# An x eviction on VectorE, a normalisation on GpSimd, and weight tiles split earlier

## The chip, the cores and the metric

The kernel runs on one core of one Trainium2 chip. The metric is the device time of one launch in microseconds (us). Before the change it was 877.35 us, the median of three runs (876.28 to 878.45). The engines are called PE (TensorE, matrix products), ACT (ScalarE), DVE (VectorE), POOL (GpSimd) and SP (SyncE, which here only issues DMAs). SBUF is the on-chip memory, PSUM the banks into which PE accumulates.

## The reference

Three stages follow one another, with B = 4, H = 8 heads of 64, 512 local and 32 global tokens for each batch.

```python
# 1. attention: local queries see a band of +-32 keys and the 32 global keys, global queries see all
out_g = sm(scale * q_g @ k_all.T) @ v_all
out_l = sm(concat(scale * q_l @ k_g.T, where(|i-j| <= 32, scale * q_l @ k_l.T, -1e9))) @ concat(v_g, v_l)
x = concat(out_g, out_l)                       # 2176 tokens x 512
# 2. gated layer, 512 -> 1536 -> 512
x = ((sigmoid(x @ w_gate) * (x @ w_val)) @ w_out)
# 3. routed layer: tokens with x @ w_skip > 0 go to the best of 8 experts (512 -> 1024 -> 512), the others pass
out = x;  out[sel] += gate_w * (relu(x[sel] @ w1[e]) @ w2[e])
```

The weights of the gated layer come as 64-bit numbers. They are turned into 32-bit words on the chip ("narrowed"), scaled by a power of two, and split into a high and a low 16-bit part, so that a product is made of three matmuls.

## The kernel before, in words

**Attention (to about 177 us).** There are 32 units, one for each tile of 128 tokens and each half of the heads. A software pipeline, written out in `MAIN` (L57), runs in each step u the scores of unit u, the softmax of the units before, the transposes of unit u-3, the value products of unit u-4, and the eviction `xout` of unit u-5. The eviction (`x_out`, L431) copies two halves of 64 partitions x 256 from PSUM (`xo`) to SBUF (`xT`) and then stores the tile; `ENG` (L55) says which engine makes each half (`x0`, `x1`: 'a' is ACT, 'v' DVE, 'p' POOL). For each batch and half of the heads the global queries have steps of their own (`globals_`, L444): a maximum, an exponential, the normalisation `norm` (L464, 128x544, engine `g_n`), transposes of it by PE (`tpg`), and value products (`xog`).

**Side steps.** Weight tiles of the gated layer are made inside the pipeline. Tile n (of 12) has three raw pieces of 512 KB, k = 3n to 3n+2 (gate, value, output). A piece is fetched (L140, SP), narrowed (three DVE passes, L156, L158, L160); of the first two the absolute sum is taken by ACT (`total_w1`, L177, output `junk`, sums in `vm`), summed over partitions by a small PE matmul (`sum_w1`, L180, output `ws`), turned into scales (`scale_w1`, four small DVE operations from L170 to L172 and L533), and split: the high part by ACT (`high_w1`, L102, `wa`, `wb`), the low part as the difference on DVE (`low_w1`, L202) or, for the third piece, on POOL (L109) where `SUBS` says so. `W_FIRST` (L51) holds the steps at which tiles 0 to 4 begin, `W_STEPS` the steps that follow.

**The tail (177 to about 205 us).** `UPS` (L60) puts the up products of weight tiles 0 to 3 for the first token block into the last steps, while the last global queries are finished. An up product of one tile is 24 matmuls of 128x512 (L570 to L572) into two banks `pp` of three; the sigmoid `sg` (ACT, L581), the product `g` (DVE, L583) and its split `gh` (ACT, L596) and `go` (DVE, L597) follow. ACT loads another function table before the first sigmoid.

**Gated layer, first block.** For each of 12 tiles (`fc`) the loop at L983 runs up (L561), gated, cut, then the sum of a later weight tile (`w1_sum`), the down product of the tile before (12 matmuls of 128x512, L609 to L611), and then `w1_make`, which scales and splits that later tile, fetches further pieces, and narrows the tile behind it (`w1_words`). Raw pieces from k = 15 on rotate over 11 places: four of pool `st`, four of `st2`, three of `rw` (L122). Tile 5 is summed and made at fc 0, tile 6 at fc 4, ..., tile 11 at fc 9. Five more token blocks follow, with all weights in place, and then the routed layer to the end of the run. Each engine works through its own instructions in the program's order.

Of the kernel before, what the change touches and what calls it, by code (L numbers as in the profile page):

```python
# [11 lines left out]
F32 = mybir.dt.float32  # L12
# [35 lines left out]
G_STEPS = [[(0, 'top'), (0.5, 'weigh'), (1.5, 'over'), (1.5, 'norm'), (2, 'turn', 0), (2.5, 'turned', 0), (3, 'turn', 1), (3.5, 'turned', 1), (4, 'value'), (4.5, 'out')], [(1, 'top'), (1.5, 'weigh'), (2.5, 'over'), (2.5, 'norm'), (5, 'turn', 0), (5.5, 'turned', 0), (6, 'turn', 1), (6.5, 'turned', 1), (7, 'value'), (7.5, 'out')]]  # L48
G_LAST = [[(0, 'top'), (0, 'weigh'), (0.5, 'over'), (0.5, 'norm'), (1, 'turn', 0), (1, 'turned', 0), (1.5, 'turn', 1), (1.5, 'turned', 1), (2, 'value'), (2.5, 'out')], [(0, 'top'), (0, 'weigh'), (0.5, 'over'), (0.5, 'norm'), (2.5, 'turn', 0), (2.5, 'turned', 0), (3, 'turn', 1), (3, 'turned', 1), (3.5, 'value'), (4, 'out')]]
W_STEPS = [(0, 'fetch', 0), (0.5, 'fetch', 1), (2.5, 'narrow', 0), (3, 'total', 0), (3, 'narrow', 1), (3.5, 'fetch', 2), (3.5, 'total', 1), (5, 'sum'), (5.5, 'scale'), (5.5, 'high', 0), (6, 'low', 0), (6, 'high', 1), (6, 'narrow', 2), (6.5, 'low', 1), (6.5, 'high', 2), (7, 'low', 2)]  # L50
W_FIRST = (4, 10, 16, 22, 28)  # L51
X_STEPS = [(16, 'load'), (17, 'total', 0), (18, 'total', 1), (19, 'total', 2), (20, 'total', 3), (22, 'sum'), (22.5, 'scale'), (23, 'part', 0), (24, 'part', 1), (25, 'part', 2), (26, 'part', 3)]
SUBS = 'vvp'
W_LOW = 'v'
ENG = {'x0': 'a', 'x1': 'a', 'g_n': 'a', 't0': 'a', 't1': 'a', 'tg': 'v'}  # L55

MAIN = [('gout', 1), ('tmm', 3), ('norm', 2), ('score', 0, 0), ('score', 1, 0), ('turned', 3), ('xout', 5), ('exp', 0, 1), ('exp', 1, 1), ('mid',), ('max', 0, 0), ('max', 1, 0), ('gmm', 0), ('val', 4), ('end',)]  # L57
STEPS = 38
TAGS = {'x': 1, 's': 2, 'pr': 3, 'sm': 2, 'pt': 2, 'xT': 2}
UPS = (33, 34, 35, 36)  # L60
EARLY = len(UPS)
# [13 lines left out]
def moe_kernel(ctx, tc, qL, kL, qG, vA, wpack, epack, wr, wrT, masks, cst, out):  # L75
# [46 lines left out]
    place = {}  # L122
    for k in range(W0, 3 * NW):
        i = (k - W0) % (sum(NST) + 3)
        name = "st" if i < NST[0] else "st2" if i < sum(NST) else "rw"
        place[k] = name, [j for j in place if place[j][0] == name]
    for k, (name, prev) in place.items():
        n = dict(rw=3, st=NST[0], st2=NST[1])[name]
# [148 lines left out]
    def at(u, f):  # L277
        if u <= -1:
            f()
        else:  # L280
            side.setdefault(u, []).append(f)
# [333 lines left out]
    def bank(name):  # L615
        banks.append(banks.pop(0))
        return mps.tile([128, 512], F32, tag=banks[-1], name=name)
# [111 lines left out]
        return steps + [r_pick, r_place]  # L729

    todo = []
    w1k = [W0, W0 // 3]

    def w1_fetch(a):

# [4 lines left out]
    def w1_words(n):  # L740
        if n < NW:
            narrow_w1(3 * n, 3 * n + 1)
            narrow_w1(3 * n + 2)
            for k in range(3 * n, 3 * n + 2):
                total_w1(k)

    def w1_sum(n):
        if n < NW:
            w1s.append(bank("ws")[:, 0:2])
            sum_w1(n, w1s[-1])  # L750

    w1s = []
# [1 line left out]
    def w1_make(n):  # L754

        if n >= NW:
            return
        scale_w1(n, w1s.pop())
        for k in range(3 * n, 3 * n + 3):
            high_w1(k)  # L760
        for k in range(3 * n, 3 * n + 3):
            low_w1(k, SUBS[k % len(SUBS)])
        w1_fetch(3 * n + 3)
        w1_words(n + 1)
        if n + 1 == NW:
            st2.close()
            pools["wpc"] = ctx.enter_context(tc.tile_pool(name="wpc", bufs=4, reuse_waits="tile"))
            st.close()
            pools["wpd"] = ctx.enter_context(tc.tile_pool(name="wpd", bufs=2, reuse_waits="tile"))
# [28 lines left out]

    for n, u0 in enumerate(W_FIRST):
        do = dict(fetch=lambda h, n=n: fetch_w1(3 * n + h), narrow=lambda h, n=n: narrow_w1(3 * n + h), total=lambda h, n=n: total_w1(3 * n + h),  # L800
                  sum=lambda n=n: side_sum(2, lambda ps: sum_w1(n, ps)), scale=lambda n=n: scale_w1(n, summed.pop()),
                  high=lambda h, n=n: high_w1(3 * n + h), low=lambda h, n=n: low_w1(3 * n + h, W_LOW))
        for r, f, *a in W_STEPS:
            at(u0 + r, lambda f=do[f], a=a: f(*a))

    do = dict(load=lambda: x_load(0), total=lambda k: x_total(0, k), sum=lambda: side_sum(4, lambda ps: x_sum(0, ps)),
              scale=lambda: x_scale(0, summed.pop()), part=lambda k: x_part(0, k))
# [37 lines left out]

    st2 = ctx.enter_context(ExitStack())
    pools["st2"] = st2.enter_context(tc.tile_pool(name="st2", bufs=NST[1], reuse_waits="tile"))
    w1_fetch(W0)
    w1_words(W0 // 3)
    mps = mp.enter_context(tc.tile_pool(name="mps", bufs=1, space=PSUM, reuse_waits="tile"))  # L850

    def gather(xr, ix):
# [118 lines left out]
    for n in range(NB):  # L971
        if n == 1:
            xs_ = ctx.enter_context(ExitStack())
            xa = xs_.enter_context(tc.tile_pool(name="xa", bufs=1, reuse_waits="tile"))
            aix = xa.tile([128, NA], I32, tag="aix", name="aix")

            zrows = xa.tile([128, XW], F32, tag="axr", name="zrows", bufs=NA)
            nc.gpsimd.memset(zrows, 0.0)
            w_rows((NE,), xa.tile([128, XW], F32, tag="axr", name="wrow", bufs=NA)[:, 0:512])
            for t in range(first_tile[NB - 1], NT):  # L980
                for r, m, row in token_rows(t):
                    nc.sync.dma_start(x1d[row:row + m, :], zrows[r:r + m])
        for fc in range(NFC):  # L983
            if n or fc >= EARLY:
                up(n, fc)
                gated(n, fc)
                cut(n, fc)
            if n == 0:
                w1_sum(max(fc, 3) + 2 if fc in (0, *range(4, NFC)) else NW)
            if n == NB - 1 and todo and fc >= 1:  # L990
                todo.pop(0)()
            if fc:
                down(n, fc - 1)
            if n == 0 and fc == 1:
                cut(0, 3)
            if n == 0 and fc == NFC - 2:

                for c in range(3):
                    w_rows((2 * c, 2 * c + 1), rw.tile([128, 1024], F32, tag="raw", name="wrow"))
                for c in (6, 7):  # L1000
                    w_rows((c,), rw.tile([128, 512], F32, tag="cut", name="wrow", bufs=2))
            if n == 0:
                w1_make(max(fc, 3) + 2 if fc in (0, *range(4, NFC)) else NW)
            if n + 1 < NB:
                if fc == 2:
                    x_load(n + 1)
                if 4 <= fc < 8:
                    x_total(n + 1, fc - 4)
                if fc == 9:
                    ps = bank("xs")[:, 0:4]  # L1010
                    x_sum(n + 1, ps)
                    x_scale(n + 1, ps)
            if todo and fc >= 1:
                todo.pop(0)()
            if n == NB - 1 and fc < NFC - 1:

                free = NR - 1 + max(0, fc - 1)
                w2_ahead(min(NW + 2 * fc, free - 1, 27), min(free, 27))
        if n + 1 < NB:
            x_split(n + 1)  # L1020
        down(n, NFC - 1)
        todo = route(n)
        if n == NB - 2:
            r_rows, t0, s0, t1, s1, t2, s2, r_pick, r_place = todo
            none = lambda: None
            todo = [r_rows, t0, t1, s0, t2, s1, s2, r_pick, none, r_place, none, a_list, a_gather] + 8 * [none] + [lambda: a_turn(0)]
        if n < NB - 1:
            todo.pop(0)()
# [360 lines left out]
```

## Time and profile before

| | |
|---|---|
| median of three runs | 877.35 us (876.28 to 878.45) |
| the profiled execution | 878.84 us, of which span 877.1 us |
| PE busy | 780.1 us (89%) |
| DVE busy | 505.7 us (58%) |
| ACT busy | 378.7 us (43%) |
| POOL busy | 72.1 us (8%) |
| DMA moved | 105.80 MB, mean 121 GB/s |

The span is the stretch that the profiler saw; the rest of the execution lies around it. The shares are means over the whole run and differ much by stage, so the stages are looked at by stretches, by the waits of PE and by the instructions in their order of time.

### The profile page before, as it was taken

The page shows a single profiled execution, that of the slowest core. Times are in us where ns is not written, and L with a number is a line of the kernel's source. Part 1 is how long each engine was busy: PE and PEld are TensorE (multiplying, and loading weights), DVE is VectorE, ACT ScalarE, POOL GpSimd, SP SyncE. Part 2 cuts the span into 40 slices and gives each one's busy share as a digit, 9 for nine tenths or more (in the row PEclk, how much of TensorE's full clock was granted, in tenths as well). Part 3 has the DMA queues.
Part 4 walks back from the last instruction along what each step waited for, and adds up shares of the span by engine and source line. Part 5 has one row for each costly group of instructions (what it writes and reads, how often), then busy time and mean ns, then how long its engine had stood idle before and what let it go on. Part 6 is the DMA issues. An engine that isn't in the chain of part 4 may idle for free. (4 is left out here: it accounts for less than half of the span.)

```text
span 877.1 us, 13434 instructions
## 1 busy us (share of the span) xinstructions
PE 780.1 (89%) x4598; PEld 595.9 (68%) x4598; DVE 505.7 (58%) x1358; ACT 378.7 (43%) x906; POOL 72.1 (8%) x95
## 2 busy tenths in 40 slices
PE   5989898997978999999999999989987576799993
PEld 5989798964644566666678866667865454578773
DVE  5576878844688557635647755336424266554731
ACT  4596979762244332131232232143423255553530
POOL 2000000000111000010000010100111201132210
PEclk9899999998998999999999999999999687899997
DMA  8988786245430230021011020034718476654300
GB/s 247 233 250 205 253 232 191 70 147 181 143 128 30 73 109 13 5 82 25 0 73 37 17 69 1 25 133 147 154 49 122 163 274 209 221 188 167 114 26 18
DMA packets 58404, 105.80 MB, mean 121 GB/s; under 512 B 10609, under 2 KB 32369, under 8 KB 57282
## 3 DMA queue, kind: packets, MB, share of 16 engines
q1 hardware_dynamic: 52386, 94.47, 36.4%
q0 software_dynamic: 3040, 6.70, 2.4%
q10 hardware_dynamic: 2880, 3.41, 1.4%
q8 instruction: 51, 0.84, 0.4%
q14 instruction: 47, 0.39, 0.2%
HBM read 87.82 MB, written 17.98 MB: 121 GB/s over the span
## 5 line engine op out<-in xcount | busy, mean ns | idle before, releaser
L570 PE MATMUL pp<-xh,wa 128*128 128x384 f16 (+2 forms) x576 | 184.9, 321 | 0.0
L572 PE MATMUL pp<-xh,wa 128*128 128x384 f16 (+2 forms) x576 | 183.9, 319 | 0.0
L571 PE MATMUL pp<-xl,wa 128*128 128x384 f16 (+2 forms) x576 | 183.8, 319 | 0.0
L583 DVE SCALAR_TENSOR_TENSOR g<-pp,inv,sg 128x384 f32<-128x384 f32 (+2 forms) x72 | 42.8, 595 | 116.9 <-PE pp L572 112.2
L581 ACT ACTIVATE sg<-pp,inv 128x384 f32<-128x384 f32 (+2 forms) x72 | 40.5, 562 | 134.8 <-PE pp L572 131.5
L609 PE MATMUL acc<-wb,gh 128*128 128x512 f32 x200 | 89.5, 448 | 0.0
L596 ACT CAST gh<-g 128x384 fp32r<-128x384 f32 (+2 forms) x71 | 35.0, 493 | 122.2 <-DVE g L583 120.8
L570 PEld LDWEIGHTS <-wa 128*128 128x128 f16 x576 | 57.3, 99 | 44.0 <-issue 15.7
L216 DVE TENSOR_TENSOR wb<-raw,wa 128x1024 fp32r<-128x1024 f32 x64 | 76.1, 1221 | 18.4 <-ACT wa L215 17.3
L610 PE MATMUL acc<-wb,gh 128*128 128x512 f32 x200 | 82.1, 411 | 0.0
L611 PE MATMUL acc<-wb,go 128*128 128x512 f32 x200 | 81.9, 410 | 0.0
L572 PEld LDWEIGHTS <-wa 128*128 128x128 f16 x576 | 56.7, 98 | 33.3 <-issue 1.2
L718 DVE CUSTOM_DVE_ANT_0 junk<-x,wrow 128x512 f32<-128x512 f32 x108 | 75.4, 698 | 2.6
L571 PEld LDWEIGHTS <-wa 128*128 128x128 f16 x576 | 56.9, 99 | 29.1 <-issue 0.8
L215 ACT CAST wa<-raw 128x1024 fp32r<-128x1024 f32 x64 | 64.9, 1047 | 14.9 <-DMA raw<-in_epack_dram 13.1
L597 DVE TENSOR_TENSOR go<-g,gh 128x384 fp32r<-128x384 f32 (+2 forms) x71 | 37.9, 534 | 39.0 <-ACT gh L596 38.6
L340 PE MATMUL sp<-k,qz 128*128 128x160 f32 x256 | 45.1, 323 | 12.5 <-DMA x1d<-zrow 5.7
L379 ACT ACTIVATE pr<-sm,st 128x160 f32<-128x160 f32 x128 | 53.2, 417 | 0.7
L424 PE MATMUL xo<-pt,g 128*128 128x128 f32 x256 | 49.8, 276 | 0.0
L340 PEld LDWEIGHTS sp<-k,qz 128*128 128x128 f32 x256 | 39.6, 207 | 13.3 <-issue 5.9
L609 PEld LDWEIGHTS acc<-wb,gh 128*128 128x128 f32 x200 | 39.6, 198 | 11.0 <-issue 1.7
L611 PEld LDWEIGHTS acc<-wb,go 128*128 128x128 f32 x200 | 39.4, 197 | 9.7
(276 smaller groups left out, 1400.4 us busy)
## 6 DMA issues: line engine op xcount, KB each, us to landing
raw<-in_epack_dram SPq DMA_DIRECT2D x64, 512.0 KB, 5.6
raw<-in_wpack_dram SPq DMA_DIRECT2D x36, 512.0 KB, 4.6
k<-in_kL_dram SPq DMA_DIRECT2D x32, 256.0 KB, 6.0
v<-in_vA_dram SPq DMA_DIRECT2D x4, 1280.0 KB
x1d<-x SPq DMA_DIRECT2D x16, 260.0 KB, 2.4
w<-in_vA_dram SPq DMA_DIRECT2D x8, 512.0 KB, 8.3
xTd<-xT SPq DMA_DIRECT2D x16, 256.0 KB, 5.3
out_dram<-x SPq DMA_DIRECT2D x16, 256.0 KB, 4.6
```

The lines of the kernel that those rows point to most:

```text
L215: nc.scalar.copy(t[0], raw)
L216: nc.vector.tensor_sub(t[1], raw, t[0])
L340: nc.tensor.matmul(sp[:, 160 - 160 * s:320 - 160 * s], q, qk[t][g][:, pp, 96 * s:96 * s + 160], start=True, stop=True)
L379: nc.scalar.activation(U[u, "pr"][:, c // 2, cs], sm[:, c // 2, cs], AF.Exp, bias=st[:, c:c + 1], scale=-1.0, accum_out=U[u, "r"][:, c:c + 1])
L424: nc.tensor.matmul(xo[:, pp, s], gf[b % 2][:, s, p], pt[:, 4], start=False, stop=True)
L570: nc.tensor.matmul(pp[:, 0:nt], hi[:, ks], xh[k][:, 0:nt], start=(k == 0), stop=False)
L571: nc.tensor.matmul(pp[:, 0:nt], hi[:, ks], xl[k][:, 0:nt], start=False, stop=False)
L572: nc.tensor.matmul(pp[:, 0:nt], lo[:, ks], xh[k][:, 0:nt], start=False, stop=(k == 3))
L609: nc.tensor.matmul(acc, gh[:, gs], hi, start=(fc == 0), stop=False)
L610: nc.tensor.matmul(acc, gh[:, gs], lo, start=False, stop=False)
L611: nc.tensor.matmul(acc, go[:, gs], hi, start=False, stop=(fc == NFC - 1))
L718: nc.vector.tensor_tensor_reduce(junk, R["x1"][:, g, 0:DM], wrow[c], op0=ALU.mult, op1=ALU.add, scale=1.0, scalar=0.0, accum_out=R["lo"][: ...
```

## The change

Five things change. The second half of each x eviction goes from ACT to DVE (32 copies of 64x256). The normalisation of the global queries goes from ACT to POOL (8 of 128x544), as a multiply by a value per partition. The first two weight tiles of the gated layer begin at steps 2 and 9 instead of 4 and 10. Tiles 5 and 6 are fetched, narrowed, summed and made by entries of a new table `W_TAIL` in the tail (steps 33.5 to 38; one step more is run); in the first block tile 7 is summed and made at fc 0, tiles 8 to 11 at fc 3 to 6, and the narrowing runs two tiles ahead: tiles 7 and 8 are narrowed ahead of the loop, and `w1_make(n)` narrows tile n+2. The raw places rotate as `st`, `rw`, `st2`.

```diff
--- before.py
+++ after.py
@@ -48,14 +48,16 @@
 G_STEPS = [[(0, 'top'), (0.5, 'weigh'), (1.5, 'over'), (1.5, 'norm'), (2, 'turn', 0), (2.5, 'turned', 0), (3, 'turn', 1), (3.5, 'turned', 1), (4, 'value'), (4.5, 'out')], [(1, 'top'), (1.5, 'weigh'), (2.5, 'over'), (2.5, 'norm'), (5, 'turn', 0), (5.5, 'turned', 0), (6, 'turn', 1), (6.5, 'turned', 1), (7, 'value'), (7.5, 'out')]]
 G_LAST = [[(0, 'top'), (0, 'weigh'), (0.5, 'over'), (0.5, 'norm'), (1, 'turn', 0), (1, 'turned', 0), (1.5, 'turn', 1), (1.5, 'turned', 1), (2, 'value'), (2.5, 'out')], [(0, 'top'), (0, 'weigh'), (0.5, 'over'), (0.5, 'norm'), (2.5, 'turn', 0), (2.5, 'turned', 0), (3, 'turn', 1), (3, 'turned', 1), (3.5, 'value'), (4, 'out')]]
 W_STEPS = [(0, 'fetch', 0), (0.5, 'fetch', 1), (2.5, 'narrow', 0), (3, 'total', 0), (3, 'narrow', 1), (3.5, 'fetch', 2), (3.5, 'total', 1), (5, 'sum'), (5.5, 'scale'), (5.5, 'high', 0), (6, 'low', 0), (6, 'high', 1), (6, 'narrow', 2), (6.5, 'low', 1), (6.5, 'high', 2), (7, 'low', 2)]
-W_FIRST = (4, 10, 16, 22, 28)
+W_FIRST = (2, 9, 16, 22, 28)
+
+W_TAIL = [(33.5, 'words', 5), (35, 'fetch'), (35.5, 'sum', 5), (36, 'make', 5), (36.5, 'words', 6), (38, 'sum', 6), (38, 'make', 6)]
 X_STEPS = [(16, 'load'), (17, 'total', 0), (18, 'total', 1), (19, 'total', 2), (20, 'total', 3), (22, 'sum'), (22.5, 'scale'), (23, 'part', 0), (24, 'part', 1), (25, 'part', 2), (26, 'part', 3)]
 SUBS = 'vvp'
 W_LOW = 'v'
-ENG = {'x0': 'a', 'x1': 'a', 'g_n': 'a', 't0': 'a', 't1': 'a', 'tg': 'v'}
+ENG = {'x0': 'a', 'x1': 'v', 'g_n': 'p', 't0': 'a', 't1': 'a', 'tg': 'v'}
 
 MAIN = [('gout', 1), ('tmm', 3), ('norm', 2), ('score', 0, 0), ('score', 1, 0), ('turned', 3), ('xout', 5), ('exp', 0, 1), ('exp', 1, 1), ('mid',), ('max', 0, 0), ('max', 1, 0), ('gmm', 0), ('val', 4), ('end',)]
-STEPS = 38
+STEPS = 39
 TAGS = {'x': 1, 's': 2, 'pr': 3, 'sm': 2, 'pt': 2, 'xT': 2}
 UPS = (33, 34, 35, 36)
 EARLY = len(UPS)
@@ -122,7 +124,7 @@
     place = {}
     for k in range(W0, 3 * NW):
         i = (k - W0) % (sum(NST) + 3)
-        name = "st" if i < NST[0] else "st2" if i < sum(NST) else "rw"
+        name = "st" if i < NST[0] else "rw" if i < NST[0] + 3 else "st2"
         place[k] = name, [j for j in place if place[j][0] == name]
     for k, (name, prev) in place.items():
         n = dict(rw=3, st=NST[0], st2=NST[1])[name]
@@ -729,7 +731,7 @@
         return steps + [r_pick, r_place]
 
     todo = []
-    w1k = [W0, W0 // 3]
+    w1k = [W0]
 
     def w1_fetch(a):
 
@@ -744,9 +746,9 @@
             for k in range(3 * n, 3 * n + 2):
                 total_w1(k)
 
-    def w1_sum(n):
+    def w1_sum(n, ps=None):
         if n < NW:
-            w1s.append(bank("ws")[:, 0:2])
+            w1s.append((bank("ws") if ps is None else ps)[:, 0:2])
             sum_w1(n, w1s[-1])
 
     w1s = []
@@ -761,7 +763,8 @@
         for k in range(3 * n, 3 * n + 3):
             low_w1(k, SUBS[k % len(SUBS)])
         w1_fetch(3 * n + 3)
-        w1_words(n + 1)
+        if n >= NWA:
+            w1_words(n + 2)
         if n + 1 == NW:
             st2.close()
             pools["wpc"] = ctx.enter_context(tc.tile_pool(name="wpc", bufs=4, reuse_waits="tile"))
@@ -802,6 +805,9 @@
                   high=lambda h, n=n: high_w1(3 * n + h), low=lambda h, n=n: low_w1(3 * n + h, W_LOW))
         for r, f, *a in W_STEPS:
             at(u0 + r, lambda f=do[f], a=a: f(*a))
+    do = dict(fetch=lambda: w1_fetch(W0), words=w1_words, sum=lambda n: w1_sum(n, aps.tile([128, 6, 128], F32, tag="tp", name="ws", bufs=1)[:, 0]), make=w1_make)
+    for u, f, *a in W_TAIL:
+        at(u, lambda f=do[f], a=a: f(*a))
 
     do = dict(load=lambda: x_load(0), total=lambda k: x_total(0, k), sum=lambda: side_sum(4, lambda ps: x_sum(0, ps)),
               scale=lambda: x_scale(0, summed.pop()), part=lambda k: x_part(0, k))
@@ -845,8 +851,9 @@
 
     st2 = ctx.enter_context(ExitStack())
     pools["st2"] = st2.enter_context(tc.tile_pool(name="st2", bufs=NST[1], reuse_waits="tile"))
-    w1_fetch(W0)
-    w1_words(W0 // 3)
+    w1_fetch(3 * NWA)
+    w1_words(NWA)
+    w1_words(NWA + 1)
     mps = mp.enter_context(tc.tile_pool(name="mps", bufs=1, space=PSUM, reuse_waits="tile"))
 
     def gather(xr, ix):
@@ -986,7 +993,7 @@
                 gated(n, fc)
                 cut(n, fc)
             if n == 0:
-                w1_sum(max(fc, 3) + 2 if fc in (0, *range(4, NFC)) else NW)
+                w1_sum(NWA + (0, NW, NW, 1, 2, 3, 4, *[NW] * 5)[fc])
             if n == NB - 1 and todo and fc >= 1:
                 todo.pop(0)()
             if fc:
@@ -1000,7 +1007,7 @@
                 for c in (6, 7):
                     w_rows((c,), rw.tile([128, 512], F32, tag="cut", name="wrow", bufs=2))
             if n == 0:
-                w1_make(max(fc, 3) + 2 if fc in (0, *range(4, NFC)) else NW)
+                w1_make(NWA + (0, NW, NW, 1, 2, 3, 4, *[NW] * 5)[fc])
             if n + 1 < NB:
                 if fc == 2:
                     x_load(n + 1)
```

Line numbers of the changed kernel are two to seven higher. On DVE at the end of the tail, before the change, the scales of tile 4 (`we`, `ws`, `inv`) are followed by the copy of the last transposed global weights (`ptg`) and the first gated product (`g`):

```order
519 L170 TENSOR_SCALAR we<-pt 128x2
520 L171 TENSOR_SCALAR we<-we 128x2
521 L172 TENSOR_SCALAR ws<-we 128x2
522 L533 TENSOR_SCALAR inv<-we,xq 128x2
523 L104 COPY ptg<-tpg 128x128
524 L583 SCALAR_TENSOR_TENSOR g<-pp,inv,sg 128x512
```

and after it:

```order
552 L535 TENSOR_SCALAR inv<-we,xq 128x2
553 L158 TENSOR_SCALAR cut<-raw 128x512 x2
554 L160 SCALAR_TENSOR_TENSOR cut<-raw,cut 128x512 x2
555 L162 SCALAR_TENSOR_TENSOR raw<-raw,cut 128x512 x2
556 L158 TENSOR_SCALAR cut<-raw 128x512
557 L160 SCALAR_TENSOR_TENSOR cut<-raw,cut 128x512
558 L162 SCALAR_TENSOR_TENSOR raw<-raw,cut 128x512
559 L106 COPY ptg<-tpg 128x128
560 L585 SCALAR_TENSOR_TENSOR g<-pp,inv,sg 128x512
```

The narrowing of tile 5 (the passes on `cut` and `raw`) now stands between the scales and `ptg`; its sums (ACT `junk`) stand ahead of ACT's table load.

On PE, at the end of the last up product of the tail (`pp`), the sum `ws` and the start of the first down product (`acc`), before:

```order
638 L572 MATMUL pp<-xh_1775,wa 128x512
639 L180 MATMUL ws<-vm,onesf 128x2
640 L609 MATMUL acc_2506<-wb,gh 128x512
641 L610 MATMUL acc_2506<-wb,gh 128x512
642 L611 MATMUL acc_2506<-wb,go 128x512
```

and after:

```order
639 L574 MATMUL pp<-xh_1775,wa 128x512
640 L182 MATMUL ws<-vm,onesf 128x2 x2
641 L611 MATMUL acc_2588<-wb,gh 128x512
642 L612 MATMUL acc_2588<-wb,gh 128x512
643 L613 MATMUL acc_2588<-wb,go 128x512
```

The one sum there was of tile 5; now there are two, of tiles 6 and 7, and the first down product stands behind both.

On DVE in the pipeline of attention, between the normalisation of a unit (`pr`, `pk`) and the masked maximum (`sm`, `st`) of a later one, with the semaphores that an instruction waits for, before:

```order
118 L388 TENSOR_TENSOR pr<-pr,r 128x2x2x128 [waits DVE_49]
119 L391 TENSOR_TENSOR pk<-pr,r 128x128
120 L351 ISA sm,st<-sp,mask_sb 128x160 [waits PE_49]
121 L351 ISA st 128x1
122 L351 ISA sm,st<-sp,mask_sb 128x160
```

and after, where the second half of the eviction (`xT`) has come in, and a low part moved:

```order
129 L390 TENSOR_TENSOR pr<-pr,r 128x2x2x128 [waits DVE_49]
130 L393 TENSOR_TENSOR pk<-pr,r 128x128
131 L106 COPY xT<-xo 64x256 [waits DMAHW6_49,PE_49,Activation_49]
132 L204 SCALAR_TENSOR_TENSOR wa<-raw,ws,wa 128x512
133 L353 ISA sm,st<-sp,mask_sb 128x160 [waits PE_49]
134 L353 ISA st 128x1
```

The new copy waits for PE and for ACT; the maxima stand behind it.

## Rows read from the trace of the kernel before

**Rows 1.** Busy time by stretch (span, then per engine: busy and count); PEclk, DMA share, GB/s.

```profile
125.00:150.00 25.00, 20.37 (x166) 19.39 (x165) 20.59 (x86) 20.06 (x63) 0.00 (x0) 1.00 0.74 219
...
sum 151.00, PE 139.18 PEld 135.23 DVE 114.66 ACT 119.41 POOL 0.00; mean PE 23.20 PEld 22.54 DVE 19.11 ACT 19.90 POOL 0.00
...
200.00:212.00 12.00, 11.40 (x52) 5.86 (x50) 2.19 (x6) 1.30 (x2) 0.00 (x0) 0.86 0.42 112
```

**Rows 2.** PE waits, 24 to 178 us: who waits for whom; total, times, longest.

```profile
PE tpg L471 <- ACT pgf L102: 4.8, 3, 2.3
```

**Rows 3.** The same for PE from 178 to 310 us.

```profile
PE ws L180 <- ACT junk L177: 13.9, 5, 5.0
```

**Rows 4.** DVE groups by form, 0 to 180 us: total busy, mean ns; idle before.

```profile
L104 DVE COPY ptg<-tpg 128x512 f32<-128x512 f32 x6 | 4.1, 683 | 0.0
...
L492 DVE COPY xTg<-xog 64x64 f32<-64x64 f32 x12 | 2.6, 220 | 1.2 <-PE xog L486 1.1
...
L104 DVE COPY ptg<-tpg 128x128 f32<-128x128 f32 x6 | 1.7, 284 | 0.0
```

**Rows 5.** ACT groups by form, same stretch: the normalisation.

```profile
L102 ACT ACTIVATE pgf<-pgf,gt 128x544 f32<-128x544 f32 x7 | 5.2, 741 | 1.6 <-DVE gt L462 1.6
```

**Rows 6.** POOL groups by form, whole run.

```profile
L109 POOL TENSOR_TENSOR wb<-raw,wb 128x512 fp32r<-128x512 f32 x7 | 9.1, 1304 | 280.3 <-ACT wb L102 270.2 <-PE pp L572 10.0
...
L978 POOL MEMSET zrows<- 128x520 f32 x1 | 0.5, 524 | 0.0
```

**Rows 7.** DVE in time order: start, duration, line, operation, count [idle before].

```profile
184.47 0.22 DVE L533 TENSOR_SCALAR inv<-we,xq 128x2 f32<-128x2 f32 x1
...
193.26 0.46 DVE L492 COPY xTg<-xog 64x64 f32<-64x64 f32 x2 [0.59 <-PE xog L486]
...
203.29 0.69 DVE L597 TENSOR_TENSOR gc<-g,gc 128x512 fp32r<-128x512 f32 x1 [0.74 <-ACT gc L596]
...
212.56 0.75 DVE L156 TENSOR_SCALAR cut<-raw 128x512 uint32<-128x512 uint32 x2
...
220.14 1.86 DVE L156 TENSOR_SCALAR cut<-raw 128x512 uint32<-128x512 uint32 x2
...
246.80 0.15 DVE L170 TENSOR_SCALAR we<-ws 128x2 f32<-128x2 f32 x1
...
249.51 1.85 DVE L156 TENSOR_SCALAR cut<-raw 128x512 uint32<-128x512 uint32 x2
...
254.87 0.69 DVE L160 SCALAR_TENSOR_TENSOR raw<-raw,cut 128x512 uint32<-128x512 uint32 x1
...
258.12 0.15 DVE L170 TENSOR_SCALAR we<-ws 128x2 f32<-128x2 f32 x1
```

**Rows 8.** ACT in time order, same columns.

```profile
185.41 1.28 ACT L581 ACT_TABLE_LOAD   x1
186.71 0.69 ACT L581 ACTIVATE sg<-pp,inv 128x512 f32<-128x512 f32 x1
...
225.27 0.20 ACT L177 ACTIVATION_READ_ACCUMULATOR junk<-raw 128x1 f32 x1
```

**Rows 9.** PE in time order, same columns.

```profile
187.88 0.38 PE L570 MATMUL pp<-xh,wa 128*128 128x512 f16 x1
...
205.24 0.63 PE L572 MATMUL pp<-xh,wa 128*128 128x512 f16 x1
...
208.60 0.38 PE L571 MATMUL pp<-xl,wa 128*128 128x512 f16 x1
...
211.41 0.38 PE L572 MATMUL pp<-xh,wa 128*128 128x512 f16 x1
216.77 0.59 PE L180 MATMUL ws<-vm,onesf 128*128 128x2 f32 x2 [4.98 <-ACT junk L177]
...
292.13 0.38 PE L570 MATMUL pp<-xh,wa 128*128 128x512 f16 x1
...
300.11 0.39 PE L570 MATMUL pp<-xh,wa 128*128 128x512 f16 x1
```

## The prediction

> **What bounds the kernel now.** I read the stretches first, then the waits of PE, then the instructions in order of time around the places that the change touches. In attention PE is the bound: it works 139.18 of the 151 us from 24 to 175, while DVE works 114.66 and ACT 119.41, 76 and 79% [rows 1]. But DVE is not far behind: from 125 to 150 it is busy 20.59 us, a little more than PE's 20.37. Of PE's few waits there the largest is for the normalisation on ACT, 4.8 us in three waits [rows 2]. From 178 to 310 PE waits 13.9 us, in five waits, for the sums of the weight tiles, whose releaser is ACT's `junk`, the last step behind the narrowing on DVE [rows 3]. There the limit is a chain on DVE and ACT: scale and low part, narrow, sum, each 11.32 us behind the one before (246.80 to 258.12, scale to scale) [rows 7], against a step of PE of 7.98 us (292.13 to 300.11) [rows 9].
>
> **The eviction.** It is 32 copies of 64x256 from PSUM. DVE's copies of 128x512 and 128x128 mean 683 and 284 ns [rows 4]; 256 elements a partition lie at a third of the way, 0.42 us. So DVE gets 32 x 0.42 = 13.4 us, and up to 16 us at 0.5 each if none overlaps its neighbours. DVE goes from 114.66 to some 129 of 151 us. The two copies of 64x64 at 193.26, one on each half of the partitions, take 0.46 us together, no less than twice their mean of 0.220 [rows 4, 7]: such a pair is not overlapped. The Trainium skill says the same ("VectorE: DVE Perf Modes", section "Two Vector instructions with no wait between them"): an instruction whose start quadrant differs from the last one's is held until all earlier Vector instructions have finished, which would hit each copy on the upper half and what follows it. By that rule the upper figure of 16 us holds, without it 13.4.
>
> The copy also waits for ACT's half, and the masked maxima, which release PE's scores, stand right behind it on DVE. Ends: nothing, if DVE's 36 us of idle time take it all, to +16 if all of it reaches PE. I charge a third, +4.5: in most stretches DVE has the time, but from 125 to 150 it has none to spare, and anywhere a copy that comes late holds the maxima behind it. ACT gets 32 short copies less, which pays only where PE waits for ACT.
>
> **The normalisation.** ACT takes 0.741 us for one [rows 5]. POOL does no such operation in this trace. The nearest rows are its memset of 128x520, 0.524, and its two-input operation on 128x512, 1.304, which for 544 elements is 1.38 [rows 6]. So one takes between 0.55 and 1.38; I take 1.0, near their middle, 0.26 longer than on ACT. Against this it no longer queues behind ACT's copies and exponentials, which is part of the 4.8 us. Ends -3 to +2; I take -1. A price on DVE belongs to it: the two DVE passes at 220.14, where POOL's operation runs beside them, take 1.86 us, those at 212.56 take 0.75 [rows 7]. The Trainium skill has the rule ("GPSIMD Engine Reference", section "Specifications"): POOL shares its SBUF interfaces with VectorE and contends with operations in a two-port mode or with two SBUF inputs. The trace agrees by that 1.1 us. If each of the eight normalisations hit DVE so and a third reached PE, the sum would be 3 us more; the end of +2 covers most of that.
>
> **The earlier first tiles.** Their raw DMAs now stand on SP's queue ahead of loads of q and k. Nothing in the rows prices this; a piece is 512 KB like the others. A piece of 512 KB at the run's mean of 121 GB/s is 4.3 us; I take a quarter of it, +1, with ends 0 and +4.3, since most loads are issued a step or more ahead of their use. Attention together: +4.5 - 1 + 1 = +4.5.
>
> **The tail.** Times here are those of before, without attention's shift. The narrowing of tile 5 now begins on DVE when the scales of tile 4 are done, at 184.47 + 0.22 = 184.69 [rows 7], and ACT has its two `junk` passes ahead of the table load. From a narrowing's start to the end of `junk` before: 220.14 to 225.47, 5.33 us beside POOL, 4.2 without the 1.1 [rows 7, 8]. So `junk` ends at 188.9, the table load and the first sigmoid need 1.99 more (185.41 to 187.40) and end at 190.9 instead of 187.40 [rows 8]. The value half of the second up product needs the bank that this sigmoid reads; it began at 187.88 [rows 9]. It waits 3.0 us.
>
> The last split of product 2 (`gc`) then ends at 203.98 + 3 = 207.0 [rows 7]. The scale and low parts of tile 5 follow, 2.71 us (246.80 to 249.51), a small copy of 0.46, and tile 6 is narrowed from 210.2, its `junk` done at 215.5. The last up product ends at 211.79 + 3 = 214.8, so the sum of tile 6 waits 0.7. But the sum of tile 7 stands right behind it on PE, ahead of the down products that are ready. On DVE: narrowing of tile 6 until 216.2 (6.05 us, 249.51 to 254.87 + 0.69), `g` 0.7 (like a 128x512 copy), scale and low of tile 6 2.71, narrowing of tile 7 from 219.6, `junk` at 224.95. PE stands still for 9.4 us, where it stood 4.98 before [rows 9], and goes on at 225.0, where it did at 216.77: 8.2 late.
>
> **The middle of block 0.** The chain on DVE continues from there: tile 7 narrowed at 225.65; tile 8, without POOL beside it, 4.9 later, 230.6; scale and low of 7, 233.3; tile 9, 239.35; `go`, scale and low of 8, 242.7; tile 10, 248.75; `g` and `go` 2.56 (255.56 to 258.12), scale and low of 9, 254.0; tile 11's `junk` at 259.35. ACT's sigmoid of product 5 stands behind that and ends at 260.5; PE's value half of up product 6 waits for it, about 3 us. From there nothing of the chain is left: half an up product, 12 x 0.216 = 2.6 (pitch from 208.60 to 211.41, 13 matmuls), the down product 7.98 - 24 x 0.216 = 2.8, so up 7 begins at 266, and up 11 after 4 x 7.98 at 297.9. Before it began at 300.11: -2. Eight us were lost at the head, but the four later waits for sums, 13.9 - 5.0 = 8.9 us, are gone, because tile 11 is narrowed at step 6 and not 9.
>
> **The clock.** From 200 to 212 the granted clock was 0.86 [rows 1], and eight matmuls from 205.24 to 208.60 took 0.42 us each, where those up to 211.41 took 0.216 [rows 9]: TensorE fell to its lower level (1.2 GHz of 2.4) after the short, broken work of the tail. Eight at the higher level take 1.7 instead of 3.4: 1.7 us. Two new stalls on PE's path, at 188 and 258, can each cost that; what the long one at 215 costs is hidden behind DVE's chain. +3, ends 0 and +5.
>
> **Sum.** +4.5 - 2 + 3 = 5.5, of which I take +5, since some of the 188 stall's price also lies before DVE's idle time. The profiled execution of before took 878.84, the runs a median of 877.35; 5 more than the median is about 882.5.
>
> **The rivals.**
> 1. *Attention hides its part.* DVE's 36 us of idle time hold the copies and the normalisation pays for the rest; left are -2 + 3, and the time is 878. For it: PE is busy 92%. Against: the copy waits for ACT, and maxima wait behind it.
> 2. *Faster: the chain starts soon enough.* If the sum of tile 7 waits no longer than the old 5.0, the 8.9 us of later waits are a clear gain: with attention's +4.5 it is -4.4, 873. For it: DVE is idle for long in the tail. Against: the narrowing of tile 6 stands behind the scales of 5, and these behind `gc`.
> 3. *Slower by more: the upper half of the copies.* DVE becomes the bound of attention: from 129 us of 151 with waits for ACT between, half of 16 us reaches PE, +8, and with the clock's drop in stretches where PE now is idle the sum is +10, 887.5. It decides where PE waits for `st` in most steps.
> 4. *The tiles end no earlier.* If `rw` places come free late (their low parts are released at the end of the tail), tile 7's words arrive late and the stall at 215 grows; +3 on the forecast, within rival 3's range.
>
> **How the numbers follow.** A measurement of this kernel can tell about 0.3%, 2.6 us, from no change. Forecast, +2.7 to +8.5: 0.47. Rivals 3 and 4, above that: 0.17. Rival 1, within 2.6 us: 0.19. Rival 2, faster: 0.17, and that takes in that the normalisation or ACT's relief pays more than -3. The range goes from 873.5 to 889.5, from rival 2's time to two beyond rival 3's; the forecast's own range is 880 to 886.
>
> **What would show it.** PE's waits up to 178 us: those for `st` should rise from a few us and those for the normalisation fall. The start of the first up product should be some 4 us later; up 2 another 3; the wait for `ws` at some 220 should be near 9 us, and no wait for `ws` should stand after it; the up product of tile 11 should begin about 2 to 3 us later than before or earlier, once attention's shift is taken off. The copies `xT` on DVE should mean 0.42 us. It is wrong if DVE's added time leaves PE's start of the first up product where it was, or if the two sums cost no more than the one did.

## The result and the profile after

The changed kernel took 887.05 us (median of ten runs, 881.25 to 889.21), the kernel before 876.39 us in the runs beside it (871.57 to 879.37): the ratio is 1.0116, with a 95% interval of 1.0088 to 1.0143. It is 10.2 us slower at 876.39, 7.7 to 12.5 by the interval. The forecast was 5 slower.

First where the time went. This is the stretch from 24 us to the first up product of the gated layer in the kernel before; the columns are those of [rows 1], with the granted clock third from the end.

```profile
24.00:176.77 152.77, 140.95 (x1153) 136.99 (x1152) 115.28 (x471) 121.18 (x399) 0.00 (x0) 0.99 0.75 206
```

The same in the changed kernel, where the first up product begins 9.2 us later:

```profile
24.00:186.01 162.01, 146.45 (x1154) 141.67 (x1155) 128.54 (x498) 102.19 (x366) 4.32 (x6) 0.96 0.69 195
```

PE runs the same matmuls in both (1153 and 1154 records) and needs 9.2 us longer. Of these, 3.7 are idle time (162.01 - 146.45 = 15.6 against 11.8), and 5.5 are busy time, for the same work: the clock was 0.96 and not 0.99, which over 162 us is 6.5 us lost against 1.5. The next view shows two places of the changed kernel where it fell.

```profile
110.00:115.00 5.00, 4.30 (x37) 3.97 (x36) 4.76 (x20) 2.99 (x13) 0.00 (x0) 1.00 0.24 65
115.00:120.00 5.00, 5.00 (x29) 4.80 (x29) 1.65 (x9) 2.63 (x11) 0.00 (x0) 0.66 0.33 96
...
150.00:155.00 5.00, 2.73 (x14) 2.73 (x15) 4.09 (x19) 2.08 (x7) 0.72 (x1) 0.78 0.55 154
```

Each fall comes with or behind a stretch in which PE had waited. In the kernel before such stretches are there too, and there the clock held:

```profile
90.00:95.00 5.00, 3.42 (x27) 2.98 (x25) 4.90 (x18) 3.37 (x13) 0.00 (x0) 1.00 0.98 355
95.00:100.00 5.00, 3.06 (x25) 2.67 (x24) 3.95 (x19) 4.94 (x16) 0.00 (x0) 1.00 1.09 340
```

Not all of this belongs to the moved copy. PE's first scores begin at 24.63 us and not at 23.15, and from 25 to 30 us the clock was 0.50 against 0.74, while the first moved copy runs at 32.39. And the kernel before is the only one of this study in whose trace the clock did not fall at all between 30 us and the first up product. The kernel that differs from the changed one by this copy alone (it stands under the experiments) shows

```profile
24.00:176.18 152.18, 142.18 (x1154) 138.82 (x1153) 115.37 (x471) 117.54 (x393) 4.33 (x6) 0.98 0.75 205
```

Against it the changed kernel has 5.6 us more idle time (15.6 and 10.0; 0.6 of it lies ahead of its first score) and 4.3 us more busy time (146.45 and 142.18): so the larger part is waiting, the smaller part clock. Over stretches of 5 us from 30 us on, the loss by the clock (length times one minus the clock) was 3.4 us in the changed kernel, 3.4 to 6.8 in the other kernels with a copy on DVE, and 1.7 or 3.4 in the others with both copies on ACT. Each of these is read from one execution.

What makes PE wait is seen on DVE. The moved copy from 24 us to the first up product of the changed kernel; mean ns, then idle time in front and its releaser:

```profile
L106 DVE COPY xT<-xo 64x256 f32<-64x256 f32 x28 | 12.0, 428 | 25.2 <-ACT xT L104 21.4 <-PE sp L342 3.5
```

The copy takes 0.428 us, as worked out. But DVE stands in front of it for 25 us, 21 of them for ACT's half. Before, DVE waited 12.5 us for the exponentials, in front of a small operation of the normalisation (`r`); this wait is gone, and DVE now waits longer, and in another place of its queue. One case in the changed kernel, first ACT in time order:

```profile
117.37 0.70 ACT L104 ACTIVATE pt<-tp 128x640 f32<-128x640 f32 x1 [4.35 <-PE tp L402]
117.97 0.37 ACT L104 ACTIVATE xT<-xo 64x256 f32<-64x256 f32 x1
```

and DVE's half behind it, with the masked maximum:

```profile
118.36 0.43 DVE L106 COPY xT<-xo 64x256 f32<-64x256 f32 x1 [3.29 <-ACT xT L104]
...
119.29 0.33 DVE L353 CUSTOM_DVE_ANT_0 sm<-sp,mask_sb 128x160 f32<-128x160 f32 x1
```

ACT's half stands behind its copy of PE's transposes (`pt`), which waits for PE. So DVE now waits for PE's transposes by way of ACT, and the maxima stand behind that. What reaches PE are these waits of its scores for the maxima (total, times, longest), before and after:

```profile
PE sp L340 <- DVE st L351: 1.8, 2, 1.3
...
PE sp L342 <- DVE st L353: 3.4, 4, 1.7
```

They rise, as forecast, but by 1.6 us only. PE's waits for the transposed global weights that DVE copies (`ptg`) rise from 1.0 to 2.7 us, those for ACT's copy of the global scores (`sgs`) from 1.5 to 2.8; those for the normalisation, which were to fall, stay (4.8 and 4.5).

The other parts. PE's waits from the first up product to the second token block of after, answering to [rows 3]:

```profile
PE ws L182 <- ACT junk L179: 11.4, 2, 9.1
PE pp L572 <- ACT sg L583: 7.8, 3, 3.6
```

and the places in time order:

```profile
200.85 0.59 PE L572 MATMUL pp<-xh,wa 128*128 128x512 f16 x1 [3.57 <-ACT sg L583]
...
236.47 0.59 PE L182 MATMUL ws<-vm,onesf 128*128 128x2 f32 x2 [9.09 <-ACT junk L179]
...
271.33 0.38 PE L572 MATMUL pp<-xh,wa 128*128 128x512 f16 x1 [2.95 <-ACT sg L583]
```

The value half of the second up product waits 3.57 us (3.0 forecast), the sum of tile 7 9.09 (9.4), the value half of up product 6 2.95 (about 3). Two more waits have less or nothing in the working: 2.36 us for the sum of tile 6 at 226.99 (0.7) and 1.29 at 260.01, in front of the value half of up product 5 (none). The up product of tile 11 begins at 310.73 instead of 300.11 [rows 9], 10.6 late; 9.2 of these were there at the first up product, so the tail and the middle together cost 1.4. This 1.4 is the rest of two larger amounts. From the first up product to the second token block, before and after:

```profile
176.77:310.90 134.13, 118.97 (x539) 71.58 (x537) 82.80 (x162) 55.89 (x108) 9.59 (x8) 0.92 0.34 114
...
186.01:321.52 135.51, 115.22 (x539) 69.75 (x537) 82.67 (x167) 51.86 (x102) 11.14 (x10) 0.92 0.33 112
```

PE's idle time rises from 15.2 to 20.3 us, 5.1 more, and its busy time falls by 3.7 for as many matmuls. Before, the clock fell behind the later waits for sums (0.66 from 256 to 261 us, 0.58 from 276 to 281, 0.74 from 281 to 286); with those waits gone it stayed at 1.00 from 276 us to the end of the block.

The normalisation on POOL takes about what it took on ACT [rows 5]:

```profile
L108 POOL TENSOR_SCALAR pgf<-pgf,gt 128x544 f32<-128x544 f32 x8 | 5.7, 719 | 178.4 <-DVE gt L464 141.1 <-DVE gt L463 31.4 <-PE tpg L473 5.8
```

### The profile page after: what moved, and what is told of

It is laid out like the page before. It is cut to its first block, busy times and chain, and to the rows that moved or that the text cites. A ratio compares the mean times of both kernels' runs of the same rounds, so it can differ in the third digit from the quotient of the medians.

```text
span 885.5 us, 13478 instructions
## 1 busy us (share of the span) xinstructions
PE 779.9 (88%) x4598; PEld 597.3 (67%) x4598; DVE 518.6 (59%) x1390; ACT 355.7 (40%) x866; POOL 77.7 (9%) x103
## 5 line engine op out<-in xcount | busy, mean ns | idle before, releaser
L611 PE MATMUL acc<-wb,gh 128*128 128x512 f32 x200 | 88.6, 443 | 0.0
L612 PE MATMUL acc<-wb,gh 128*128 128x512 f32 x200 | 80.7, 404 | 0.0
L217 ACT CAST wa<-raw 128x1024 fp32r<-128x1024 f32 x64 | 64.9, 1048 | 13.8 <-DMA raw<-in_epack_dram 11.9
L701 POOL DMA_INDIRECT lst<-tok,pi x17 | 16.9, 992 | 372.2 <-DVE cum L705 321.2
```

The costliest lines, as they stand in the source:

```text
L217: nc.scalar.copy(t[0], raw)
L611: nc.tensor.matmul(acc, gh[:, gs], hi, start=(fc == 0), stop=False)
L612: nc.tensor.matmul(acc, gh[:, gs], lo, start=False, stop=False)
```

## The experiments

Every kernel was timed in five rounds against the kernel before; times are medians, ratios have 95% intervals. Theory A: the moved copy ties DVE to ACT in the middle of its queue. B: the early raw loads hold up loads of q. C: the copy's own time on DVE. D: the loss is the tail's.

**The upper half on DVE alone.**

```diff
-ENG = {'x0': 'a', 'x1': 'a', 'g_n': 'a', ...
+ENG = {'x0': 'a', 'x1': 'v', 'g_n': 'a', ...
```

> The kernel before with one edit: the upper half of each x eviction on DVE. Attention lost 9.2 us in the changed kernel's trace (first up product at 186.0 instead of 176.8), where 4.5 was forecast. Theory A (this copy waits for ACT's half, and DVE's maxima wait behind it): +5 to +8 us against before, DVE idle some 20 us in front of the copies. Rival B (the raw pieces fetched earlier hold up loads of q and k): this edit alone +2 to +4, idle time much the same. The forecast's own term was +4.5.

Measured: 888.14 us, before 879.12; ratio 1.0108 (1.0057 to 1.0158), +9.5 us. This one edit makes about the whole loss (5.0 to 13.9 by the interval). B falls as an explanation of it. PE from 24 us to the first up product, at 188.8:

```profile
24.00:188.78 164.78, 148.98 (x1153) 144.21 (x1152) 128.52 (x498) 106.29 (x372) 0.00 (x0) 0.94 0.70 191
```

The copies on DVE in the same kernel:

```profile
L104 DVE COPY xT<-xo 64x256 f32<-64x256 f32 x27 | 11.5, 428 | 26.6 <-ACT xT L102 21.4 <-PE sp L340 4.8
```

Of the 12.0 us by which it is later, 4.0 are idle time and 8.0 busy time, with the clock at 0.94: the same two parts as in the changed kernel.

**The lower half on DVE instead.**

```diff
-ENG = {'x0': 'a', 'x1': 'a', 'g_n': 'a', ...
+ENG = {'x0': 'v', 'x1': 'a', 'g_n': 'a', ...
```

> The kernel before with the lower half of each x eviction on DVE instead of the upper one. DVE gets as many copies of the same size, but it is now ACT's copy that waits for DVE's. Theory A (the wait for ACT is the cost): 0 to +3 us, at least 3 less than with the upper half. Rival C (the copy's own 0.43 us on DVE is the cost): within 1.5 us of the kernel with the upper half.

Measured: 885.54, ratio 1.0076 (1.0043 to 1.0108), +6.7 us. Inconclusive: 2.8 us less than the upper half, too near to tell apart by these intervals, and more than A expected. The waiting only changed sides, as ACT's group shows:

```profile
L102 ACT ACTIVATE xT<-xo 64x256 f32<-64x256 f32 x28 | 10.6, 379 | 18.1 <-DVE xT L104 17.5
```

ACT now stands 17.5 us for DVE's half, in the middle of its own queue. That test did not take the tie away; the next does.

**Both halves on DVE.**

```diff
-ENG = {'x0': 'a', 'x1': 'a', 'g_n': 'a', ...
+ENG = {'x0': 'v', 'x1': 'v', 'g_n': 'a', ...
```

> The kernel before with both halves of each x eviction on DVE: 64 copies there, some 27 us of DVE time, twice as many as with one half, and no copy that waits for the other engine. Theory A (what costs is that one engine stands still in the middle of its queue until the other has made its half; in the kernel with the upper half on DVE its copies are preceded by 20 us of idle time): -1 to +4 us against before, less than the 6.7 of the kernel with the lower half on DVE alone. Theory C (the copy's own time on DVE): +12 or more.

Measured: 884.28, before 878.69; ratio 1.0064 (1.0037 to 1.0092), +5.6 us (3.3 to 8.1). Twice the copies cost no more than one half of them did, and half of what theory C needs; but also more than A allowed. The copies on DVE:

```profile
L104 DVE COPY xT<-xo 64x256 f32<-64x256 f32 x56 | 23.4, 419 | 2.7 <-PE xo L424 2.2
```

There is hardly any waiting in front of them, and 23.4 us of work. That what is left of the loss comes from that work is likely, but not shown: PE's idle time up to the first up product is 14.9 us, and its clock 0.96.

**The upper half on DVE, behind the maxima.**

```diff
-... ('turned', 3), ('xout', 5), ('exp', 0, 1), ('exp', 1, 1), ('mid',), ('max', 0, 0), ('max', 1, 0), ('gmm', 0), ...
+... ('turned', 3), ('exp', 0, 1), ('exp', 1, 1), ('mid',), ('max', 0, 0), ('max', 1, 0), ('xout', 5), ('gmm', 0), ...
```

> The kernel before with the upper half of each x eviction on DVE, and the eviction of a step moved behind the maxima of that step, so that no maximum stands behind a copy that waits for ACT. Theory A: most of the 9.5 us of the unmoved kernel goes, +1 to +5 is left (the copy still holds what follows it on DVE). Theory C: +8 to +11, as without the move.

Measured: 881.98, ratio 1.0041 (1.0012 to 1.007), +3.6 us. The same copies on the same engine, in another place, cost 6 us less by the medians; the intervals (5.0 to 13.9, and 1.1 to 6.2) overlap a little. ACT's half moved too, behind the exponentials. In its profile

```profile
L104 DVE COPY xT<-xo 64x256 f32<-64x256 f32 x28 | 12.0, 428 | 12.4 <-ACT xT L102 11.9
```

the wait in front is halved, and what stands behind it is no longer what PE's scores wait for: their waits for the maxima are 0.6 us in this trace, against 2.1 with the copy in its first place. PE's idle time up to the first up product is 12.0 us, that of before:

```profile
24.00:184.22 160.22, 148.24 (x1153) 144.46 (x1154) 129.65 (x498) 106.11 (x373) 0.00 (x0) 0.94 0.72 199
```

but the clock is 0.94 and PE's busy time 7.3 us longer in this one execution. Kernels with both copies on ACT lie between 0.96 and 0.99, so what of this belongs to the edit stays open.

**The other two edits in attention, each alone.** The early first tiles, and the normalisation on POOL:

```diff
-W_FIRST = (4, 10, 16, 22, 28)
+W_FIRST = (2, 9, 16, 22, 28)
```

> The kernel before with one edit: the first two weight tiles begin at steps 2 and 9 instead of 4 and 10. Rival B (raw pieces in front of loads of q and k): +4 to +6 us, with longer waits of PE for the loads of q in the first 60 us. Theory A: within 2 us of before. The forecast's own term was +1.

Measured: 877.50, before 879.12; ratio 0.9974 (0.9946 to 1.0003), -2.3 us. B falls. (PE's first scores begin at 23.5 to 24.6 us in the traces of the six kernels with this edit and at 23.1 to 23.9 in the other seven: if the first loads of q came later, it was by half a us or so.)

```diff
-ENG = {'x0': 'a', 'x1': 'a', 'g_n': 'a', ...
+ENG = {'x0': 'a', 'x1': 'a', 'g_n': 'p', ...
```

> The kernel before with one edit: the normalisation of the global queries on POOL. Forecast's own term -1, ends -3 to +2. In the changed kernel's trace one took 0.719 us on POOL (0.741 on ACT before). Theory A: -2 to +1. A rival, that POOL's port takes time from DVE's two-input passes beside it: +1 to +4.

Measured: 877.78, before 877.93; ratio 0.9983 (0.9952 to 1.0015): no difference that can be measured, and of the rival's +1 to +4 the interval leaves only what lies below +1.3.

**The tail and the middle alone, and the changed kernel without the moved copy.**

```diff
 # changed kernel
-W_FIRST = (2, 9, 16, 22, 28)
+W_FIRST = (4, 10, 16, 22, 28)
-ENG = {'x0': 'a', 'x1': 'v', 'g_n': 'p', ...
+ENG = {'x0': 'a', 'x1': 'a', 'g_n': 'a', ...
```

> The changed kernel without its three edits in attention (both x halves and the normalisation on ACT, the first tiles begin at steps 4 and 10): what is left is the tail and the middle of block 0. From the two traces these cost +5.3 from the first to the third up product, +5.3 to the fifth, and gave back 9.2 to the twelfth: +1.4 in all. Theory A and the forecast's terms (-2 and +3): -1 to +3. A rival D, that the loss is made in the tail and only seems to be attention's: +6 or more.

Measured: 878.93, before 879.12; ratio 0.9990 (0.9957 to 1.0023), -0.9 us. D falls.

```diff
 # changed kernel
-ENG = {'x0': 'a', 'x1': 'v', 'g_n': 'p', ...
+ENG = {'x0': 'a', 'x1': 'a', 'g_n': 'p', ...
```

> The changed kernel with the upper half of the eviction back on ACT, all else as changed: normalisation on POOL, first tiles early, tail and middle of block 0. If the eviction carries the whole loss (9.5 us alone), this lies 8 to 12 us under the changed kernel, at -4 to +1 against before: the early first tiles gave -2.3 and the tail -0.9 alone. If the parts work on each other (the early loads hurt more with POOL or a fuller DVE), +3 or more is left.

Measured: 877.57, before 878.69; ratio 0.9981 (0.9954 to 1.0007), -1.7 us. With the copy back on ACT the loss is gone: in the changed kernel the copy is worth 11.9 us (+10.2 against -1.7).

**The tail's stall and the sums, mended.** The change's own idea, sums and narrowing ahead of need, has two stalls of PE in it. The first kernel moves tile 5's narrowing behind the second up product, the second moves the sums, makings and narrowings of block 0 to later places, the third does both. All have the eviction on ACT.

```diff
-W_TAIL = [(33.5, 'words', 5), (35, 'fetch'), ...
+W_TAIL = [(35, 'words', 5), (35, 'fetch'), ...
```

> The changed kernel with the eviction back on ACT and one more edit: tile 5 is narrowed at step 35 instead of 33.5, behind the second sigmoid, so that its sums on ACT no longer stand ahead of the function table. The forecast's step for the tail (a first sigmoid 3.5 us late, PE 3.0 us idle for it): the third up product begins 3 to 5 us earlier relative to the first than in the kernel without this edit, and the whole gains 2 to 4 us on it (-3 to -6 against before). Rival: the stall only moves to the next step, 0 to -1.5 against the kernel without this edit.

Measured: 871.37, before 877.93; ratio 0.9927 (0.9893 to 0.9961), -6.4 us. The third up product begins 20.9 us behind the first (178.20, 199.05); without the edit it was 25.7 (176.18, 201.89) and before 19.4. The stall did not move on, it went: PE has no wait for a sigmoid before the third up product.

```diff
+SUM_AT = {4: 7, 5: 8, 7: 9, 8: 10, 9: 11}      # fc: tile; MAKE_AT is the same
+WORDS_AT = {1: 8, 4: 9, 6: 10, 8: 11}
-        if n >= NWA:
-            w1_words(n + 2)
...
-    w1_words(NWA)
-    w1_words(NWA + 1)
+    w1_words(7)
...
-                w1_sum(NWA + (0, NW, NW, 1, 2, 3, 4, *[NW] * 5)[fc])
+                w1_sum(SUM_AT.get(fc, NW))
...
-                w1_make(NWA + (0, NW, NW, 1, 2, 3, 4, *[NW] * 5)[fc])
+                w1_make(MAKE_AT.get(fc, NW))
+                w1_words(WORDS_AT.get(fc, NW))
```

> The changed kernel with the eviction back on ACT, the tail as changed, and the sums and makings of tiles 7 to 11 in block 0 at fc 4, 5, 7, 8 and 9 (with the narrowings at fc 1, 4, 6 and 8), as in the kernel that moved both. If the wait for the sum of tile 7 ahead of ready down products is the larger part of what that kernel gained: -8 to -13 us against before. If the tail's stall is the larger part: -3 to -7.

Measured: 866.78, before 877.93; ratio 0.9868 (0.9818 to 0.9919), -11.6 us. The sums are the larger part.

Both edits together, with tile 6 narrowed half a step earlier as well (`(36, 'words', 6)`):

> The changed kernel with the eviction back on ACT, tile 5 narrowed one and a half steps later (behind the second up product, so that the function table and the first sigmoids do not wait for its sums), and in block 0 the sums and makings of tiles 7 to 11 at fc 4, 5, 7, 8 and 9 instead of 0, 3, 4, 5 and 6, each narrowing at a later fc (tile 8 at 1, 9 at 4, 10 at 6, 11 at 8). The waits of PE for sums (11.4 us) and for sigmoids (7.8 us) of the changed kernel should mostly go; what bounds the first block is then PE itself. Expected: -9 to -16 us against before. If the middle is bound by DVE's total work instead and not by where PE waits, -4 or less.

Measured: 861.55, before 878.69; ratio 0.9807 (0.9767 to 0.9848), -17.0 us: faster than both kernels of this study. The parts add up: -6.4 and -11.6 include the -1.7 of the kernel without either, and -1.7 - 4.7 - 9.9 = -16.3; the half step of tile 6 was not run by itself. PE's waits from 166 to 320 us:

```profile
PE ws L185 <- ACT junk L182: 3.2, 3, 2.0
```

Against 11.4 for sums in the changed kernel little is left, and none of the 7.8 for sigmoids. The second token block begins at 296.9 us; before it began at 310.9, in the changed kernel at 321.5.

## Why the prediction was right in direction and too small

The time lies in the stated range, but above the forecast's own 880 to 886, in the part to which rivals 3 and 4 together gave 0.17.

**The bound.** Right: PE bounds attention, and it lost by waits and by its clock, not by work.

**The eviction.** This is the step that was off. The term "+4.5" measured +9.5 alone (5.0 to 13.9), which is nearly the whole difference to the forecast, and 11.9 in the company of the other edits. (The four parts alone sum to 9.5 - 1.5 - 2.3 - 0.9 = +4.8, not to +10.2; their intervals are wide enough for that.) The copy's duration was right (0.43), its mechanism too (it waits for ACT, the maxima stand behind it). I charged a third of the copies' time, from 13.4 to 16 us. The runs show three other amounts. The first is the place in the queue: moving the copy behind the maxima takes 6 of the 9.5 away by the medians, +3.6 left. The second is the clock, which the forecast's sum did not have in attention at all: 4.3 us of busy time on PE beside 5.6 of idle time, against the kernel that differs by the copy alone. Rival 3 had it, "with the clock's drop in stretches where PE now is idle", at 887.5, and that is the time that came, but not by its way: it had put the bound on DVE's sum of work, which the kernel with both halves on DVE speaks against (23.4 us of copies for +5.6), and PE waits for `st` in four steps, not in most. Which part of the clock's loss follows from which wait was not tested by itself.

The third is what a copy takes of DVE's time, which is more than its duration. The upper half on DVE alone, between the operation in front and the maximum behind:

```profile
45.47 0.28 DVE L391 TENSOR_TENSOR pk<-pr,r 128x128 f32<-128x128 f32 x1
45.79 0.43 DVE L104 COPY xT<-xo 64x256 f32<-64x256 f32 x1
46.25 0.33 DVE L351 CUSTOM_DVE_ANT_0 sm<-sp,mask_sb 128x160 f32<-128x160 f32 x1
```

and the lower half on DVE alone:

```profile
43.59 0.28 DVE L391 TENSOR_TENSOR pk<-pr,r 128x128 f32<-128x128 f32 x1
43.79 0.41 DVE L104 COPY xT<-xo 64x256 f32<-64x256 f32 x1
44.12 0.31 DVE L351 CUSTOM_DVE_ANT_0 sm<-sp,mask_sb 128x160 f32<-128x160 f32 x1
```

Without a copy, what follows `pk` starts 0.20 us behind it, before `pk` has ended. With the lower half it starts 0.53 behind, with the upper half 0.78: there neither the copy nor what follows it starts before the one in front has ended. So an upper half takes some 0.57 us of DVE's time and a lower half 0.34 (medians over the cases without a wait), 18 and 11 us for 32 copies, where the working had 13.4 to 16. The quadrant rule of the Trainium skill ("VectorE: DVE Perf Modes", section "Two Vector instructions with no wait between them"), by which the copy on the upper half and what follows it are each held until the earlier instructions have finished, agrees with these starts; the mean durations, 428 and 409 ns, do not show it. It may be why the lower half cost 2.8 us less, which the runs cannot tell from nothing. With both halves on DVE a pair takes 0.88 us, 28 us for 32 pairs, and cost 5.6: at that price 18 us would be 3.6 us, an estimate, and as much is left with the copy behind the maxima.

**The normalisation.** Forecast -1 of -3 to +2; alone -1.5 (-4.2 to +1.3), not told from nothing. It takes 719 ns on POOL; I had 1.0 us.

**The early tiles.** Forecast +1; alone -2.3 (-4.7 to +0.3). The sign was probably wrong: if the loads of q suffered in this place, it cost nothing that can be measured.

**Tail, middle, clock.** -2 + 3 = +1 forecast, +1.4 in the trace, -0.9 (-3.8 to +2.0) alone. The three stalls were each within 0.6 us of the working, but the sum of tile 6 waited 2.36 and not 0.7, and 1.29 at up product 5 was not in it. The third up product is 5.3 us later relative to the first: 3.57 of stall, the rest the clock, since the eight matmuls behind the stall took 0.42 each. The four sum waits that are gone (2.00, 2.84, 1.27 and 2.85, together 9.0 us) did not make all of that good, as the working had it: the new waits are 14.3 us (3.57, 2.36, 1.29, 2.95, and 4.1 more for the sum of tile 7 than the head had before), and PE's idle time rose by 5.1. What came back is 3.7 us of busy time, by the clock that no longer fell behind those sums. The forecast had a gain by the waits and a loss by the clock, the trace shows the opposite, and that +1 and +1.4 agree is luck. (Tile 11 is made at step 6, as the working says, but narrowed at step 4, before at 8.)

**The rest of the run.** From the second token block to the end the instructions are the same in all these kernels, and that stretch took from 561.1 us (upper half on DVE alone) to 570.2 us (early first tiles alone) in their profiled executions. So single executions differ by 9 us there alone; the changed kernel's span is 8.4 us longer than that of before though its second token block begins 10.6 later, and that difference means nothing.

## What to carry to other kernels

When an operation is moved to the engine that has time, ask what it waits for there and what stands behind it: a copy of 0.43 us that waits for a sister copy on another engine ties two queues together, and ahead of the maxima it cost 9.5 us, behind them 3.6. Read what it takes of the engine from the starts of its neighbours with and without it, not from its duration: here 0.57 us and not 0.43. Charge the clock where new short waits of the matrix engine appear, not only at the long stalls, but take its size from more than one execution: here kernels with and without the copy overlap at 3.4 us. And a sum that is placed early in the matrix engine's queue is a wait in front of everything that is ready behind it: work ahead on the feeding engines, but leave the consumer where its input is surely there.

## What was not expected of the hardware

The granted clock did not follow the amount of idle time. Before, PE idled 1.58 and 1.94 us in the two stretches from 90 to 100 and kept a clock of 1.00; in the changed kernel it idled 0.70 us from 110 to 115, and 115 to 120 ran at 0.66. With an idle time as before (12.0 us against 11.8), the kernel with the late copy ran at 0.94 and not 0.99; with less, 8.3 us, the kernel with only the normalisation on POOL ran at 0.96. What decides it these runs do not show.

The multiply by a value per partition took 719 ns for 128x544 on POOL, less than ACT's 741, and much less than POOL's two-input operation on 128x512 [rows 6].
